# The convolution's second transform on four quarters of TensorE, with K's exchanged rows copied inside SBUF

## The chip, the cores and the metric

The kernel runs on one core of one Trainium2 chip. The metric is the time of one execution on the device in microseconds (us); lower is better. A core has a matrix engine (TensorE, PE in the profile, with its weight loads listed apart as PEld), a vector engine (VectorE, DVE), a scalar engine (ScalarE, ACT), a GpSimd engine (POOL) and a sync engine (SyncE, SP) that here only issues transfers. They share an on-chip memory of 128 partitions (SBUF). TensorE writes into a second, small memory of eight banks (PSUM), from which VectorE and ScalarE read. Transfers run on 16 DMA engines; SP, ACT and POOL each have a queue to issue them from.

## The reference, cut to what matters

Two mixers see the same `x` (2048 x 448) and are blended by a gate. One is a long convolution with a kernel K built from a state-space model; the other is attention within four segments of 512 rows, with a memory carried between segments.

```python
P = jnp.exp((A * dt[:, None])[:, :, None] * pos[None, None, :])
K = 2.0 * jnp.einsum("dn,dnl->dl", C, P).real          # 448 x 2048
Kf = jnp.fft.rfft(K, L2); Uf = jnp.fft.rfft(u_t, L2)   # L2 = 4096
y = jnp.fft.irfft(Uf * Kf[None, :, :], L2)[:, :, :L]
a = y + u * D_skip
...                                                     # b: attention, 16 heads of 28, 4 segments
return g * a + (1 - g) * b
```

All arithmetic is float32.

## The kernel before, in words

The first half (to about 445 us) builds K, projects q, k and v, and takes the first of two transform stages for u. The second half (`second_half`, L1206) runs the attention and, stirred into it, the rest of the convolution.

The 4096-point transform is split into two factors. The first factor leaves, in DRAM, two arrays `GU` and `GK` of 64 blocks; a block has 64 rows (real and imaginary part of 32 points) of 448 channels. `convolve` (L569) takes them through the second factor, multiplies the spectra and goes back through the inner factor of the inverse. It works in 32 chunks of two blocks, 128 rows, and has three kinds of step:

- **T**, `transform(c)`: K's chunk. Two products, one for each block, each with a 64 x 128 matrix out of `cf` and 64 x 448 data, into one PSUM buffer of two banks. ScalarE copies all 128 x 896 to `ks`. The 128 columns hold each output row twice, the second time with real and imaginary part exchanged (for K: imaginary, real, and so on), since a complex product needs both.
- **P**, `product(c)`: the same with u's chunk (real, imaginary, real, imaginary), and VectorE multiplies the PSUM buffer by `ks` into `pr` (128 x 896).
- **B**, `back(c)`: for two chunks, four products with 128 x 64 matrices out of `cb`; ScalarE copies the result to `bs`, and ACT's queue writes it to `BB` in DRAM, from where `finish` takes it at the end.

A float32 product appears in the trace as two matmul instructions. A matmul on fewer than 128 rows or columns uses a part of the array, its `tile_position`; T and P use two halves of 64 rows, B two halves of 64 columns.

The order on TensorE is written out: `mm` (L1378) keeps program order. `second_half` walks over 16 groups `i` (four segments times four groups of heads), each in six rounds `r` (L1261 to L1316). A round issues a few dummy matmuls in rounds 3, 4 and 5 (`WARM`: 1, 3, 3 of them, output `ps_pv<-wz`), one step of the next group's score maxima (`maxima`, L974; called M below), one step of this group's scores and exponentials (`weigh`, L1008; W), in round 1 the product with the values (`ps_pv<-PT,V`) and a transposition, after each segment steps of `seg_end` (L1147), which ends with 128 x 448 products by `wo`, and last some steps of `convolve`: for i from 1 to 12 an account grows by `RATIO` = 1.15 a round, and each whole unit is one step (T, P or B). What is left after i = 12 runs at once. M, W, T, P and B all draw their PSUM buffer from one ring of three (`ps("a")`, two banks each): a new one waits until the buffer three before it has been read. VectorE reads M's and P's, ScalarE W's, T's and B's. The scores come in three shapes: rounds 0 and 1 have 512 columns, 2 and 3 have 384 + 128, 4 and 5 have 256.

The order on the other engines and queues is chosen by a planner that simulates the program; only some SP transfers are tied behind others: the loads of `skip` (`xt`) behind the latest load of `gu` (`late`, `ldma`, L1408 to L1416). Loads of `gk` and `gu` come from SP through a ring of four buffers each; `cf` and `cb` are loaded once for four chunks, two buffers each.

Of the kernel before, what the change touches and what calls it, by code (L numbers as in the profile page):

```python
# [12 lines left out]
F32 = mybir.dt.float32  # L13
# [3 lines left out]
AF = mybir.ActivationFunctionType  # L17
ALU = mybir.AluOpType
# [5 lines left out]
D = 448  # L24
# [15 lines left out]
def host_consts():  # L40
# [3 lines left out]
    e = np.zeros((2, 64, 3, 512), np.float32)  # L44
    w = np.zeros((16, 3, 16, 64), np.float32)
# [3 lines left out]
    w = np.zeros((16, 3, 16, 32), np.float32)  # L49
# [4 lines left out]
    w = np.zeros((8, 2, 3, 2, 8, 32), np.float32)  # L54
# [20 lines left out]


    lane = np.arange(32)
    fw = np.zeros((64, 2, 32, 6, 32))
    bk = np.zeros((64, 4, 32, 2, 32))
    for k1 in range(64):  # L80
        k = k1 + 128 * lane
# [20 lines left out]
        f[:, :, 2:] = f[:, :, [0, 1, 1, 0]]  # L102
    fw = fw.reshape(32, 128, 192).transpose(1, 0, 2)
    bk = bk.reshape(64, 128, 64).transpose(1, 0, 2)


    f = np.stack([2 * np.cos(ang.T), -2 * np.sin(ang.T)], 1) / 4096
# [460 lines left out]

def convolve(nc, k, fp):  # L569

    NC = 32
    KB = 4
    cf, cb, gk, gu, ks, pr = {}, {}, {}, {}, {}, {}
    rows = lambda t, c: t[2 * c : 2 * c + 2].rearrange("s r n d -> (s r n) d")

    def load(c):
        if c >= NC:
            return
        if c % KB == 0:
            cf[c // KB] = fp.tile([128, KB, 192], F32, tag="cf", name="cf", bufs=2)  # L580
            k.dma(cf[c // KB], k.c_fw[:, c : c + KB])
            cb[c // KB] = fp.tile([128, 2 * KB, 64], F32, tag="cb", name="cb", bufs=2)
            k.dma(cb[c // KB], k.c_bk[:, 2 * c : 2 * c + 2 * KB])
# [5 lines left out]
    def second(c, x, o):  # L589

        pt = k.ps("a")
        w = cf[c // KB]
# [5 lines left out]
    def transform(c):  # L598
        pt = second(c, gk.pop(c), 64)
        ks[c] = fp.tile([128, 2, D], F32, tag="ks", name="ks", bufs=3)  # L600
        nc.scalar.activation(ks[c], pt, AF.Copy)

    def product(c):
        pt = second(c, gu.pop(c), 0)
        pr[c] = fp.tile([128, 2, D], F32, tag="pr", name="pr", bufs=3)
        nc.vector.tensor_tensor(pr[c], pt, ks.pop(c), ALU.mult)  # L606

    def back(c):

        pt = k.ps("a")  # L610
        for i in range(2):
            for s in range(2):
                k.mm(
                    pt[64 * s : 64 * s + 64, i, :D], cb[c // KB][:, 2 * ((c + i) % KB) + s], pr[c + i][:, s],
                    start=True, stop=True, tile_position=(0, 64 * s),
                )
            pr.pop(c + i)
        bs = fp.tile([128, 2, D], F32, tag="bs", name="bs", bufs=2)
        nc.scalar.activation(bs, pt[:, :, :D], AF.Copy)
        k.adma(k.BB[2 * c : 2 * c + 4].rearrange("(i s) r n d -> (s r n) i d", i=2), bs)  # L620

    for c in range(3):
        load(c)
    yield
    for c in range(NC + 2):
        load(c + 3)
        if c < NC:
            transform(c)
        yield
        if 1 <= c <= NC:  # L630
            product(c - 1)
            yield
        if c >= 2 and c % 2 == 1:
            back(c - 3)
            yield


# [983 lines left out]
```

## Time and profile before

| What | Value |
|---|---|
| time, median of 3 runs | 852.42 us (850.0 to 855.2) |
| span of the profiled execution, first to last instruction | 850.4 us |
| PE busy in the span | 750.1 us, 88% |
| DVE, ACT, POOL busy | 582.0, 538.6, 171.8 us |
| instructions | 19021 |
| first step T to last step B of the convolution | about 491 to 750 us |

The profiled execution's own time, apart from its span, is not listed; its span lies within the range of the times. "Busy" is the union of an engine's instructions. Matmuls overlap in the pipeline, so the distance between the starts of two blocks, not the length of one record, is what a block costs. In rows of the timeline the first number is the start in us, the second the length; a bracket gives the idle time of that engine before it and what ended it. In groups, `x` is the count, after the bar stand the busy time (us), the mean of one (ns), and the idle time before.

### The profile page before, as it was taken

The page shows a single profiled execution, that of the slowest core. Times are in us where ns is not written, and L with a number is a line of the kernel's source. Part 1 is how long each engine was busy: PE and PEld are TensorE (multiplying, and loading weights), DVE is VectorE, ACT ScalarE, POOL GpSimd, SP SyncE. Part 2 cuts the span into 40 slices and gives each one's busy share as a digit, 9 for nine tenths or more (in the row PEclk, how much of TensorE's full clock was granted, in tenths as well). Part 3 has the DMA queues.
Part 4 walks back from the last instruction along what each step waited for, and adds up shares of the span by engine and source line. Part 5 has one row for each costly group of instructions (what it writes and reads, how often), then busy time and mean ns, then how long its engine had stood idle before and what let it go on. Part 6 is the DMA issues. An engine that isn't in the chain of part 4 may idle for free.

```text
span 850.4 us, 19021 instructions
## 1 busy us (share of the span) xinstructions
PE 750.1 (88%) x7608; PEld 405.1 (48%) x7608; DVE 582.0 (68%) x1143; ACT 538.6 (63%) x638; POOL 171.8 (20%) x217
## 2 busy tenths in 40 slices
PE   1686987998879989899988999989997998988997
PEld 1363655764546655566643444434443444343443
DVE  8878678767788676876687765656565757563474
ACT  4867889799998989898863255554453444521320
POOL 5314111011110111001110121341115113331110
PEclk9589999999999989799999899999999999979899
DMA  9347853325642346314558967667466645654872
GB/s 248 91 108 237 247 186 112 99 91 172 197 143 85 104 153 200 132 46 149 178 202 349 349 221 235 204 220 233 118 219 220 194 152 182 210 205 152 223 231 97
DMA packets 88290, 152.98 MB, mean 180 GB/s; under 512 B 20626, under 2 KB 57162, under 8 KB 88154
## 3 DMA queue, kind: packets, MB, share of 16 engines
q1 hardware_dynamic: 79130, 140.83, 51.7%
q10 hardware_dynamic: 7424, 9.18, 3.1%
q0 software_dynamic: 1648, 1.76, 0.8%
q8 instruction: 60, 0.98, 0.5%
q14 instruction: 28, 0.23, 0.1%
HBM read 90.87 MB, written 60.63 MB: 178 GB/s over the span
## 4 chain that ended last, share of the span: by engine, by line
PE 54%; ACT 16%; DVE 15%; DMA 7%; issue 6%; POOL 1%; SPq 1%; ACTq 0%; DVEq 0%; POOLq 0%
PE ps_a L1379 19%; PE ps_m L1379 17%; PE ps_pv L1379 8%; ACT cs L1344 7%; PE ps_arg L1379 5%; PE ps_k L1379 3%; DVE jk L994 3%; DVE Y L397 2%; ACT L1344 2%; PE ps_m L1382 2%; DVE Y L398 1%; DVE X L393 1%; DMA xt<-in_A_u 1%; ACT EX L1344 1%; DMA ident<-in_c_id 1%
## 5 line engine op out<-in xcount | busy, mean ns | idle before, releaser
L994 DVE CUSTOM_DVE_ANT_0 jk<-ps_a,mk 128x512 f32<-128x512 f32 (+3 forms) x256 | 124.9, 488 | 71.0 <-PE ps_a L1379 63.7
L1024 ACT ACTIVATE PT<-ps_a 128x1024 f32<-128x1024 f32 (+1 forms) x96 | 84.5, 881 | 118.6 <-PE ps_a L1379 112.0
L359 POOL TENSOR_TENSOR EX<-EX,cab 128x1024 f32<-128x1024 f32 x28 | 53.5, 1913 | 309.1 <-ACT EX L1344 244.8
L1344 ACT ACTIVATE cs<-ps_arg 128x1024 f32<-128x1024 f32 x111 | 107.3, 1021 | 0.6 <-DVE Y L398 0.3
L1379 PE MATMUL ps_m<-xh,w 112*128 112x512 f32 x256 | 92.9, 412 | 0.4 <-DVE lo L765 0.4
L1379 PE MATMUL ps_a<-qu,ku 32*128 32x512 f32 (+3 forms) x768 | 89.3, 353 | 1.7 <-DVE mx L994 1.4
L1035 POOL TENSOR_SCALAR_AFFINE_SELECT PT<-PT 128x256 f32<-128x256 f32 (+1 forms) x96 | 46.5, 485 | 206.5 <-ACT PT L1024 206.4
L393 DVE TENSOR_TENSOR X<-EX,cs 128x1024 f32<-128x1024 f32 x56 | 68.3, 1220 | 25.4 <-ACT cs L1344 25.4
L1379 PE MATMUL ps_k<-Y,X 128*32 128x64 f32 x3584 | 64.1, 226 | 9.0 <-DVE Y L398 8.8
L1379 PEld LDWEIGHTS ps_k<-Y,X 128*32 128x32 f32 x3584 | 54.9, 113 | 35.2 <-DVE Y L398 16.1
L397 DVE TENSOR_TENSOR Y<-EY,cs 128x1024 f32<-128x1024 f32 x56 | 70.0, 1250 | 0.0
L1379 PEld LDWEIGHTS ps_a<-qu,ku 32*128 32x128 f32 x768 | 62.4, 194 | 12.4 <-DVE mx L994 4.7
L1344 ACT ACTIVATE cs<-cs,bhp 128x1024 f32<-128x1024 f32 x56 | 64.5, 1151 | 1.8
L399 DVE SCALAR_TENSOR_TENSOR Y<-EY,cs 128x512 f32<-128x512 f32 x56 | 41.0, 732 | 31.2 <-ACT cs L1344 29.1
L1344 ACT ACTIVATE EY<-ps_arg 128x1024 f32<-128x1024 f32 x52 | 53.1, 1031 | 11.1 <-PE ps_arg L1379 10.1
L1379 PEld LDWEIGHTS ps_m<-xh,w 112*128 112x128 f32 x256 | 48.0, 188 | 19.7 <-issue 7.6
L1379 PE MATMUL ps_a<-ku,qu 32*128 32x512 f32 (+3 forms) x256 | 46.0, 394 | 12.3 <-DVE mx L994 9.9
L1379 PE MATMUL ps_arg<-ct,lh 64*128 64x512 bf16 x224 | 43.6, 387 | 9.0 <-ACT cs L1344 5.7
L1379 PE MATMUL ps_m<-xl,w 112*128 112x512 f32 x128 | 50.3, 393 | 0.0
L1379 PEld LDWEIGHTS ps_a<-ku,qu 32*128 32x128 f32 x256 | 22.2, 189 | 58.7 <-DVE mx L994 27.0
L1379 PEld LDWEIGHTS <-lh 64*128 64x128 bf16 x392 | 22.2, 95 | 53.4 <-issue 39.8
L606 DVE TENSOR_TENSOR pr<-ps_a,ks 128x896 f32<-128x896 f32 x32 | 34.8, 1087 | 17.7 <-PE ps_a L1379 17.0
(212 smaller groups left out, 1395.3 us busy)
## 6 DMA issues: line engine op xcount, KB each, us to landing
w<-WD SPq DMA_DIRECT2D x32, 448.0 KB, 4.7
qu<-QD SPq DMA_DIRECT2D x16, 512.0 KB
ku<-KD SPq DMA_DIRECT2D x16, 512.0 KB
GU<-gs SPq DMA_DIRECT2D x32, 224.0 KB, 2.5
GK<-gs SPq DMA_DIRECT2D x8, 896.0 KB, 5.1
gk<-GK SPq DMA_DIRECT2D x32, 224.0 KB, 4.7
gu<-GU SPq DMA_DIRECT2D x32, 224.0 KB, 3.7
BB<-bs ACTq DMA_DIRECT2D x16, 448.0 KB, 2.6
```

The source lines that it names most:

```text
L359: nc.gpsimd.tensor_tensor(o, o, cab, ALU.mult)
L393: v.tensor_tensor(X, ex, t[:, :, 0], ALU.mult)
L397: v.tensor_tensor(Y[:, :, :, :32], lo, y[:, :, :, ::-1], ALU.mult)
L398: v.tensor_tensor(Y[:, 0, :, 32:], ey[:, :, 32:], y[:, 0], ALU.mult)
L399: v.scalar_tensor_tensor(Y[:, 1, :, 32:], ey[:, :, 32:], -1.0, y[:, 1], ALU.mult, ALU.mult)
L606: nc.vector.tensor_tensor(pr[c], pt, ks.pop(c), ALU.mult)
L994: v.tensor_tensor_reduce(junk[:, :n], pt[:, x, o : o + n], k.mk[:, SEG - n :], 1.0, -3e38, ALU.add, ALU.max, mx[:, 3 - t, h : h + 1],)
L1024: nc.scalar.activation(PT[:, 2 * hp : 2 * hp + 2, 512 * b : 512 * b + n], pt[:, :, :n], AF.Exp, scale=SCALE)
L1035: nc.gpsimd.affine_select(sl, sl, pat, ALU.is_ge, 0.0, base=0, channel_multiplier=-1)
L1344: x = op(*args, **kw)
L1379: tc.keep_in_program_order(nc.tensor.matmul(*args, **kw))
L1382: tc.keep_in_program_order(nc.tensor.transpose(*args))
```

## The change

T and P take two chunks at a time (`m` of 16 instead of `c` of 32) and make each output row once. The matrix is now 64 x 64, and the four products (two row halves `s`, two chunks `i`) each sit on one quarter of the array, at (64 s, 64 i). The result, for two chunks, fills one PSUM buffer as one chunk's did.

Since the exchanged rows of K are no longer made by TensorE, T copies the PSUM buffer into half 0 of `ks`, and two transfers from ACT's queue move it inside SBUF into half 1 with neighbouring partitions exchanged (even rows to odd ones, odd to even). P reads its PSUM buffer twice: two multiplications on VectorE, by half 0 and half 1. B takes `pr` in those halves: eight products of 64 x 64 on four quarters, two accumulated into each output, where there were four of 128 x 64.

`gk` and `gu` come as 16 loads of twice the size each, through rings of two; they are issued after P instead of at the start of a turn. `cf` has a third of the bytes. `ks` and `pr` have rings of two double-size buffers. The steps are 49 instead of 83, and `RATIO` is 0.68 instead of 1.15, so that they spread over the same rounds. The rest of the program, the dummies included, is untouched.

```diff
-    fw = np.zeros((64, 2, 32, 6, 32))
+    fw = np.zeros((64, 2, 32, 2, 32))
...
-    rows = lambda t, c: t[2 * c : 2 * c + 2].rearrange("s r n d -> (s r n) d")
+    rows = lambda t, m: t[4 * m : 4 * m + 4].rearrange("(i s) r n d -> (s r n) i d", i=2)
+    halves = [slice(0, 64), slice(64, 128)]
...
-        gk[c] = fp.tile([128, D], F32, tag="gk", name="gk", bufs=4)
-        k.dma(gk[c], rows(k.GK, c))
-        gu[c] = fp.tile([128, D], F32, tag="gu", name="gu", bufs=4)
-        k.late(k.dma(gu[c], rows(k.GU, c)))
+        gk[m] = fp.tile([128, 2, D], F32, tag="gk", name="gk", bufs=2)
+        k.dma(gk[m], rows(k.GK, m))
+        gu[m] = fp.tile([128, 2, D], F32, tag="gu", name="gu", bufs=2)
+        k.late(k.dma(gu[m], rows(k.GU, m)))
...
-        for s in range(2):
-            r = slice(64 * s, 64 * s + 64)
-            k.mm(pt[:, s, :D], w[r, c % KB, o : o + 128], x[r], start=True, stop=True)
+        for s, r in enumerate(halves):
+            for i, o in enumerate(halves):
+                k.mm(
+                    pt[o, s, :D], w[r, 2 * (m % 2) + i], x[r, i],
+                    start=True, stop=True, tile_position=(64 * s, 64 * i),
+                )
...
-        nc.scalar.activation(ks[c], pt, AF.Copy)
+        nc.scalar.activation(ks[m][:, 0], pt, AF.Copy)
+        x = ks[m].rearrange("(e a) b s d -> a e b s d", a=2)
+        for a in range(2):
+            k.adma(x[a, :, 1], x[1 - a, :, 0])
...
-        nc.vector.tensor_tensor(pr[c], pt, ks.pop(c), ALU.mult)
+        x = ks.pop(m)
+        for b in range(2):
+            nc.vector.tensor_tensor(pr[m][:, b], pt, x[:, b], ALU.mult)
...
-        for i in range(2):
-            for s in range(2):
-                k.mm(
-                    pt[64 * s : 64 * s + 64, i, :D], cb[c // KB][:, 2 * ((c + i) % KB) + s], pr[c + i][:, s],
-                    start=True, stop=True, tile_position=(0, 64 * s),
-                )
+        for b in range(2):
+            for i, r in enumerate(halves):
+                for s, o in enumerate(halves):
+                    k.mm(
+                        pt[o, i, :D], w[r, b, s], x[r, b, s],
+                        start=(b == 0), stop=(b == 1), tile_position=(64 * i, 64 * s),
+                    )
...
+    for m in range(NM + 2):
+        if m < NM:
+            transform(m)
             yield
+        if 1 <= m <= NM:
+            product(m - 1)
+            load(m + 1)
+            yield
+        if m >= 2:
+            back(m - 2)
             yield
...
-RATIO = 1.15
+RATIO = 0.68
```

More of the change, by code (lines that the diff above doesn't have):

```diff
@@ new lines, in transform, with product @@
+    def transform(m):
+        pt = second(m, gk.pop(m))
+        ks[m] = fp.tile([128, 2, 2, D], F32, tag="ks", name="ks", bufs=2)
+        nc.scalar.activation(ks[m][:, 0], pt, AF.Copy)
+        x = ks[m].rearrange("(e a) b s d -> a e b s d", a=2)
+        for a in range(2):
+            k.adma(x[a, :, 1], x[1 - a, :, 0])
+    def product(m):
+        pt = second(m, gu.pop(m))
+        pr[m] = fp.tile([128, 2, 2, D], F32, tag="pr", name="pr", bufs=2)
+        x = ks.pop(m)
+        for b in range(2):
+            nc.vector.tensor_tensor(pr[m][:, b], pt, x[:, b], ALU.mult)
@@ L622, in convolve @@
-    for c in range(3):
-        load(c)
+        k.adma(k.BB[4 * m : 4 * m + 4].rearrange("(i s) r n d -> (s r n) i d", i=2), bs)
+    load(0)
+    load(1)
     yield
[L625 to L631, printed above, removed]
-            yield
-        if c >= 2 and c % 2 == 1:
-            back(c - 3)
+    for m in range(NM + 2):
+        if m < NM:
+            transform(m)
+            yield
+        if 1 <= m <= NM:
[4 more added lines that the diff above has]
+            back(m - 2)
```

37 lines of the change are left out of this document (14 added, 23 removed).

## The prediction

> **What bounds the kernel now.** I read the page first: the span, the engines, and TensorE's granted clock in 40 slices of 21.3 us.
>
> ```profile
> span 850.4 us, 19021 instructions
> ...
> PE 750.1 (88%) x7608; PEld 405.1 (48%) x7608; DVE 582.0 (68%) x1143; ACT 538.6 (63%) x638; POOL 171.8 (20%) x217
> ...
> PEclk9589999999999989799999899999999999979899
> ```
>
> TensorE (PE) is the busiest, and from slice 24 on, where the convolution's steps lie (490 to 750 us), its clock is nearly always full. So the second view is that stretch alone: busy time by engine (PE, PEld, DVE, ACT, POOL in this order), then the chain that ended last, then PE's own waits.
>
> ```profile
> 490.00:750.00 260.00, 244.28 (x1746) 109.58 (x1744) 156.18 (x469) 124.00 (x151) 71.95 (x123) 0.97 0.61 197
> ...
> by line: PE ps_a L1379 42.2%; PE ps_pv L1379 16.0%; PE ps_m L1379 11.1%; DVE jk L994 4.1%; issue 4.0%; DMA xt<-in_A_u 3.7%; DMA r<-RD 2.2%; DMA dn<-pvs 2.0%; PE ps_m L1382 1.8%; DMA RD<-rs 1.6%; DMA qu<-mn 1.6%; POOL xt L1122 1.5%; DVE xt L
> ...
> PE ps_a L1379 <- DVE mx L994: 10.1, 10, 3.5
> PE ps_a L1379 <- DVE pr L606: 2.9, 6, 1.3
> ```
>
> PE is busy for 244.3 of 260 us, VectorE (DVE) for 156.2, ScalarE (ACT) for 124.0. The chain runs over PE for 42.2 + 16.0 + 11.1 + 1.8 = 71% of the stretch. What PE lost to VectorE is 10.1 + 2.9 = 13.0 us. TensorE is the limit here, and time taken from it should come back unless something else is late next. The groups by shape tell what the convolution costs, in order of cost: score maxima (`jk`), the multiplication (L606), the matmuls of T (`gk`) and B (`pr`; P's are as many as T's), and ScalarE's copy (L601).
>
> ```profile
> L994 DVE CUSTOM_DVE_ANT_0 jk<-ps_a,mk 128x512 f32<-128x512 f32 x64 | 44.0, 687 | 14.6 <-PE ps_a L1379 13.2
> ...
> L994 DVE CUSTOM_DVE_ANT_0 jk<-ps_a,mk 128x384 f32<-128x384 f32 x64 | 35.5, 554 | 30.1 <-PE ps_a L1379 28.4
> ...
> L606 DVE TENSOR_TENSOR pr<-ps_a,ks 128x896 f32<-128x896 f32 x32 | 34.8, 1087 | 17.7 <-PE ps_a L1379 17.0 <-ACT PT L1024 0.7
> ...
> L1379 PE MATMUL ps_a<-gk,cf 64*128 64x448 f32 x128 | 34.2, 612 | 2.0 <-DVE pr L606 1.3 <-DVE mx L994 0.2
> ...
> L1379 PE MATMUL ps_a<-pr,cb 128*64 128x448 f32 x128 | 30.0, 593 | 1.7 <-DVE pr L606 1.5
> L601 ACT ACTIVATE ks<-ps_a 128x896 f32<-128x896 f32 x32 | 29.3, 917 | 13.6 <-PE ps_a L1379 13.1 <-PE ps_pv L1379 0.5
> ...
> L994 DVE CUSTOM_DVE_ANT_0 jk<-ps_a,mk 128x256 f32<-128x256 f32 x64 | 27.0, 422 | 24.3 <-PE ps_a L1379 22.1 <-DVE mx L994 0.5
> ...
> L994 DVE CUSTOM_DVE_ANT_0 jk<-ps_a,mk 128x128 f32<-128x128 f32 x64 | 18.4, 288 | 2.0
> ```
>
> And the timeline gives the distance from one block to the next on PE:
>
> ```profile
> 596.73 0.18 PEld L1379 LDWEIGHTS ps_a<-ku,qu 32*128 32x128 f32 x2 [0.65 <-issue]
> ...
> 597.75 3.27 PE L1379 MATMUL ps_m<-wo,pvs 128*128 128x448 f32 x8
> ...
> 612.83 0.33 PEld L1379 LDWEIGHTS <-wz 128*128 128x128 bf16 x3 [0.65 <-issue]
> ...
> 613.58 0.18 PEld L1379 LDWEIGHTS ps_a<-ku,qu 32*128 32x128 f32 x2 [0.42 <-issue]
> ...
> 614.13 0.30 PEld L1379 LDWEIGHTS ps_a<-gk,cf 64*128 64x128 f32 x4
> ...
> 615.09 0.18 PEld L1379 LDWEIGHTS ps_a<-ku,qu 32*128 32x128 f32 x2 [0.65 <-DVE mx L994]
> ...
> 617.16 0.50 PE L1379 MATMUL ps_a<-ku,qu 32*128 32x512 f32 x2
> ...
> 618.13 2.36 PE L1379 MATMUL ps_pv<-PT,V 128*32 128x512 f32 x32
> ...
> 620.95 1.72 PE L1379 MATMUL ps_a<-pr,cb 128*64 128x448 f32 x8
> ...
> 622.61 0.18 PEld L1379 LDWEIGHTS ps_a<-ku,qu 32*128 32x128 f32 x2 [0.70 <-issue]
> ...
> 623.67 0.37 ACTq L620 DMA_DIRECT2D BB<-bs  x1
> ...
> 624.08 1.02 ACT L1024 ACTIVATE PT<-ps_a 128x1024 f32<-128x1024 f32 x1 [0.44 <-PE ps_a L1379]
> ```
>
> A T runs from 614.13 to the next block's weight load at 615.09: 0.96 us. Its record, four matmul instructions, shows that both 64-row halves run together: four of mean 612 ns fit into that distance. B takes 620.95 to 622.61, 1.66 us. A round's M and W take 617.16 to 618.13 = 0.97 us with 512 columns, 596.73 to 597.75 = 1.02 us with 384 + 128, and 613.58 to 614.13 = 0.55 us with 256; three dummies take 612.83 to 613.58 = 0.75 us.
>
> **The change, part by part.**
>
> *T and P on quarters.* 128 instructions of `gk`, four to a block, are 32 T's, and the 32 multiplications are 32 P's: 64 blocks. 32 remain, of eight instructions each. If four quarters run abreast as two halves do, a block keeps its 0.953 us (0.96 here, 0.95 for a P), and 32 x 0.953 = 30.5 us go. The trace has halves abreast by rows (T) and by columns (B), and no block with both; the bounds of the gain are 30.5 us, and for two abreast 64 x 0.953 - 32 x 1.70 = 6.6 us (a block of 2 x 0.75 us of streaming, 0.75 being the 0.95 less 0.2 of lead-in, and that 0.2). I take 30.5, since the halves in both directions show no loss.
>
> *B on quarters.* Sixteen instructions instead of eight, four abreast instead of two: the same 1.66 us, nothing changed; two abreast, they would stream 2.9 us instead of 1.46, 16 x 1.46 = 23 us more.
>
> *ScalarE.* 16 copies of 917 ns go (-14.7 us) and 32 transfers to issue come. The one that it issues now, `BB<-bs`, takes 0.37 us at 623.67, and the next instruction starts 0.41 us after it: 32 x 0.41 = 13.1 us. The sum is nothing, and ScalarE's idle 136 us cover it. Behind the two issues waits the next exponential, 0.82 us instead of the 0.92 of a copy that is gone. If the second transfer had to wait for the first to land, ScalarE would stand 2.6 us (landing of `BB<-bs`, an estimate for the exchange) 16 times; its idle time is 8.5 us to each of the 16 turns, so that too would be hidden mostly. Taken at nothing, between -1.6 us (the difference of the two sums) and +42 (16 x 2.6).
>
> *Transfers.* The exchange moves 16 x 448 KB inside SBUF. P needs it four steps after T, at 0.68 a round 5.9 rounds; 72 rounds in 260 us are 3.6 us each, so 21 us. The transfers of now, with KB each and us to landing:
>
> ```profile
> gk<-GK SPq DMA_DIRECT2D x32, 224.0 KB, 4.7
> gu<-GU SPq DMA_DIRECT2D x32, 224.0 KB, 3.7
> BB<-bs ACTq DMA_DIRECT2D x16, 448.0 KB, 2.6
> ```
>
> A load of `gk` can go once the T two turns back has read its buffer, a load of `gu` once its P has, with three steps (16 us) to spare; SP has 32 fewer issues, and queued behind them are the loads of `qu` and `ku` for later groups. At nothing: the cover is 16 us or more, against landings of 2.6 to 4.7. Were it gone, each turn would wait such a landing, 16 x 2.6 = 42 us and more.
>
> *VectorE, and the ring of three buffers.* VectorE's work is unchanged, 32 multiplications of 1087 ns, but they now come in pairs on one PSUM buffer. What that hold does is seen here:
>
> ```profile
> 542.42 1.09 DVE L606 TENSOR_TENSOR pr<-ps_a,ks 128x896 f32<-128x896 f32 x1 [0.38 <-PE ps_a L1379]
> ...
> 543.57 0.65 PE L1379 MATMUL ps_a<-gk,cf 64*128 64x448 f32 x2 [0.36 <-DVE pr L606]
> ```
>
> The multiplication ends at 543.51 and the T that wanted its buffer starts at 543.57. A multiplication starts some 0.25 us after PE has left P, so a P's buffer is free about 1.4 us after it now, and 0.25 + 2 x 1.12 = 2.5 us after it in the change (1.12 with the distance to the next). PE in the meantime does one M and W (0.55 to 1.02 us) and any dummies, and the third buffer drawn is P's. Then the next W wants the buffer of an M whose maxima VectorE could only start after the pair (1.44 us for 512 columns, 1.77 for 384 + 128, 0.93 for 256, from the groups with 0.05 us between). With RATIO 0.68 the n-th step falls in round n / 0.68, rounded up, and P of turn k is step 3k + 2 (the first is 3), which places all 16. Seven lie in quiet groups i, where no other work lies between: after P0 and P3 (round 4, a step follows) 0.75 + 0.55 us of PE work stand against 2.5, loss 1.2 each; P1 (round 1) 1.5; P8 (round 2) 1.2; P2 (round 5, no step in the next round) 1.5 for the buffer and 1.2 for the maxima behind it, 2.7; P14 (round 4, none next) 1.2 + 0.7 = 1.9; P13 (round 0) none, the values' product and the transposition, 618.13 to 620.95 = 2.8 us, cover it. Sum 9.7 us. The other nine lie in groups with segment ends, where blocks of `wo` (3.27 us at 597.75) or the waits of the next part cover them: nothing. Bounds: nothing, and 16 x 2.7 = 43 us.
>
> In sentences apart: the Trainium skill, TensorEngine Tiling (Array Packing), section Performance Considerations, says that tiling speeds up TensorE and not the reading of PSUM, which may become the bottleneck after it. By that rule the upper bound is the nearer one, and the rival "hold" below results; the groups above (VectorE idle for 104 of 260 us) bear it out in part only.
>
> *Stretches that PE doesn't set.* In four places the chain leaves PE for transfers of a segment's end (`xt`, `dn`, then `RD` and `r`). One piece of the first, then PE's work on `cf` in each of the four (four instructions to a block):
>
> ```profile
> 550.06 5.47 DMA xt<-in_A_u
> ...
> 549.70:565.30 15.60, 4.93 (x16) 1.41 (x16) 0.89 0.75 257
> 639.10:650.60 11.50, 3.07 (x12) 0.90 (x12) 1.00 0.78 270
> 711.30:720.80 9.50, 2.05 (x8) 0.60 (x8) 0.93 0.39 122
> 738.40:752.20 13.80, 1.53 (x4) 0.30 (x4) 0.88 0.39 128
> ```
>
> 16 + 12 + 8 + 4 instructions are 10 of the 64 blocks; their share, 10 / 64 x 30.5 = 4.8 us, is not gained. 0 to 10 us (10 if shorter rounds uncover as much again). In the first, `xt` is held behind a `gu` load that comes earlier now; up to 2 us less, not counted.
>
> *The clock.* PE is granted half speed in stretches of 3.41 us after a stretch in which it did little:
>
> ```profile
> 644.37:647.78 3.41, 1.98 (x13) 0.64 (x11) 1.64 (x8) 1.02 (x1) 1.65 (x2) 1.00 1.05 385
> 647.78:651.19 3.41, 1.24 (x12) 0.76 (x14) 3.38 (x8) 0.60 (x1) 3.41 (x4) 1.00 0.37 137
> 651.19:654.60 3.41, 3.41 (x10) 0.75 (x6) 0.14 (x2) 0.92 (x1) 1.66 (x4) 0.51 0.24 41
> ```
>
> 1.98 us of work in the first stretch left the clock at 1.00 in the second, the 1.24 us of the second let it fall to 0.51 in the third. Half speed for 3.41 us costs up to 1.7 us. The stalls of 2.7 and 1.9 us above leave 0.7 and 1.5 us of work, below or at that edge, those of 1.2 don't: 2 x 1.7 = 3.4 us. Bounds: 0, and 16 x 1.7 = 27 us. By the Trainium skill (TensorE: Matmul & The Clock Gate, Part 1) it takes an idle window of about 3.4 us to halve the clock, and this term would be nothing, the sum 837; the trace disagrees, with half speed after a stretch with 1.24 us of work.
>
> *Sum.* 850.4 - 30.5 + 9.7 + 4.8 + 3.4 = 837.8 us of span. The median of the runs is 2.0 us above the profiled span (852.4 against 850.4), so I predict 840 us, 1.5% less.
>
> **The rivals.**
>
> *All of the saving arrives.* VectorE is idle 40% of the stretch, and PE's waits for single products were 2.9 us; if the planner lets other maxima go between the pair, terms of 9.7 and 3.4 vanish: 850.4 - 30.5 + 4.8 + 2 = 827 us. Against it: 542.42 shows a step that waits for one product already.
>
> *The hold eats it (slower).* If each P costs PE on average more than (30.5 - 4.8) / 16 = 1.6 us, nothing is gained. At the 2.7 us of a P without a step behind it, half of them with a half-speed stretch, it is 852.4 - 30.5 + 4.8 + 43 + 14 = 884 us at the far end; at 2.2 us and five such stretches, 852.4 - 25.7 + 35 + 8.5 = 870. I put this case at 855 to 872. For it: without the 30.5 us VectorE's 156 us stand against 230 instead of 260, 68%, and its work comes in lumps.
>
> *The quarters don't run four abreast.* T and P give only 6.6 us, and B costs 23 more: 852.4 - 6.6 + 23 = 869 us, the stalls being covered by the longer blocks.
>
> *The exchange blocks ScalarE or comes late.* At the 2.6 us of a landing in each turn, 852.4 - 25.7 + 42 = 869 us. Against it: 16 us or more of cover.
>
> **How the numbers follow.** Forecast (832 to 848): 0.35. All of it arrives (823 to 832): 0.21. The hold eats it: 0.24, of which 0.08 near 852. Not four abreast: 0.07. Exchange: 0.06. The rest, 0.07, is small losses around no change. About 0.5% (4.3 us) is what a measurement of this kernel can tell from no change: faster 0.55, same 0.14, slower 0.31. The range 824 to 869 leaves out 1 in 10 at each end; the likeliest case's own is 832 to 848.
>
> **What would show it.** T, P and B of about 0.95, 0.95 and 1.66 us with 8, 8 and 16 matmul records each; the exchange landed before P; PE waiting for `pr` some 1.2 us after a P and for `mx` once behind it; half speed in quiet groups only behind stalls of 1.9 us and more. It is wrong if a T takes 1.7 us, if PE's waits on `pr` and `mx` come to more than 30 us between 490 and the last B, or if ScalarE's exponentials wait for a transfer.

## The result, and the profile after

The changed kernel takes 862.4 us (median of 4 runs, 859.58 to 864.83) where the kernel before, run beside it, takes 851.62: a ratio of 1.0124 (95% interval 1.0082 to 1.0167), 1.2% slower, about 10.6 us. I had predicted 840 us, 1.5% faster.

First the page of the changed kernel: span, engines, and TensorE's granted clock in 40 slices.

```profile
span 857.9 us, 19214 instructions
...
PE 736.7 (86%) x7736; PEld 400.1 (47%) x7736; DVE 581.9 (68%) x1143; ACT 524.4 (61%) x622; POOL 171.2 (20%) x217
...
PEclk9998999999999989899999989989996997878799
```

TensorE is busy for 13.4 us less (750.1 before) and the span is 7.5 us longer. Next the convolution's stretch, 475 to 775 us, in one row each: busy time of PE, PEld, DVE, ACT and POOL, then the mean granted clock. First the kernel before:

```profile
475.00:775.00 300.00, 279.20 (x1942) 127.29 (x1942) 179.80 (x547) 137.15 (x167) 78.90 (x136) 0.94 0.64 210
```

and the kernel after:

```profile
475.00:775.00 300.00, 257.57 (x2049) 117.64 (x2049) 175.88 (x545) 120.22 (x148) 77.19 (x133) 0.90 0.68 227
```

PE is busy for 21.6 us less, and all of that is idle time now: 42.4 us instead of 20.8. The clock fell from 0.94 to 0.90, so by estimate some 12 us more of the 300 were lost to half speed (300 x 0.04); what PE still does takes longer for it. VectorE and ScalarE have no more to do than before.

The steps themselves came out as the prediction had them. Groups by shape, kernel after:

```profile
L613 DVE TENSOR_TENSOR pr<-ps_a,ks 128x896 f32<-128x896 f32 x32 | 33.3, 1082 | 13.9 <-PE ps_a L1387 9.5 <-ACT mn L1012 3.3 <-ACT PT L1032 1.0
...
L1387 PE MATMUL ps_a<-gk,cf 64*64 64x448 f32 x128 | 16.5, 587 | 1.0 <-PE ps_a L1387 1.0
```

T's matmuls fell from 34.2 us to 16.5 with the same count of instructions: the four quarters run abreast. Now the timeline of a T and a P in a quiet group, kernel after (start, length, engine; the bracket is the idle time before and what ended it):

```profile
524.10 0.98 PE L1387 MATMUL ps_a<-gk,cf 64*64 64x448 f32 x8
...
525.01 0.33 PEld L1387 LDWEIGHTS <-wz 128*128 128x128 bf16 x3 [0.70 <-issue]
...
525.14 0.92 ACT L603 ACTIVATE ks<-ps_a 128x896 f32<-128x896 f32 x1 [0.34 <-PE ps_a L1387]
...
526.09 1.13 ACTq L606 DMA_DIRECT2D ks<-ks  x2
...
526.33 0.98 PE L1387 MATMUL ps_a<-gu,cf 64*64 64x448 f32 x8
...
527.27 0.60 ACT L1032 ACTIVATE PT<-ps_a 128x512 f32<-128x512 f32 x1 [1.21 <-PE ps_a L1387]
...
527.45 2.09 DVE L613 TENSOR_TENSOR pr<-ps_a,ks 128x896 f32<-128x896 f32 x2 [0.36 <-PE ps_a L1387]
527.92 0.53 PEld L1387 LDWEIGHTS ps_a<-qu,ku 32*128 32x128 f32 x6 [0.50 <-ACT PT L1032]
...
529.68 0.49 PE L1387 MATMUL ps_a<-ku,qu 32*128 32x512 f32 x2 [0.79 <-DVE pr L613]
...
530.93 0.96 PE L1387 MATMUL ps_a<-qu,ku 32*128 32x512 f32 x6 [0.76 <-DVE mx L1002]
```

A T costs PE 0.91 us (524.10 to 525.01) and does two chunks. But ScalarE, which ends the copy at 526.06, issues two transfers until 527.22 and only then turns to the exponential of a block that lay ready: PE's next W waits for that buffer (0.50). Then the pair of multiplications, 527.45 to 529.54, makes PE wait 0.79 us for `pr` and 0.76 for `mx`. PE's waits from 490 to 755 us, in all, how often, longest:

```profile
PE ps_a L1387 <- DVE mx L1002: 20.9, 14, 5.0
...
PE ps_a L1387 <- DVE pr L613: 4.3, 5, 1.1
PE ps_a L1387 <- ACT PT L1032: 4.2, 6, 1.7
```

Before, those for `mx` and `pr` were 10.1 and 2.9, and exponentials (`PT`) were not among what PE's matmuls waited for; its weight loads waited 1.4 us for them, and 7.6 now. The longest wait, 5.0 us, lies at a segment's end, here in the kernel after:

```profile
641.32 0.54 POOL L1107 DMA_DIRECT2D dn<-pvs  x1 [1.70 <-ACT pvs L1063]
...
642.90 0.29 DVE L1002 CUSTOM_DVE_ANT_0 jk<-ps_a,mk 128x128 f32<-128x128 f32 x1
...
648.74 0.55 DVE L1072 RECIPROCAL rc<-dn 128x64 f32<-128x64 f32 x1 [5.54 <-DMA dn<-pvs]
...
649.70 0.55 DVE L1002 CUSTOM_DVE_ANT_0 jk<-ps_a,mk 128x384 f32<-128x384 f32 x1
...
651.58 0.58 PE L1387 MATMUL ps_a<-ku,qu 32*128 32x256 f32 x2 [5.00 <-DVE mx L1002]
```

VectorE stands 5.54 us at the reciprocal `rc`, until its denominators `dn` have landed. The maxima that come behind it in VectorE's order, whose scores PE has long written, start only then (649.70), PE fills the ring of three buffers and stands too.

### The profile page after: what moved, and what is told of

Its sections match the earlier page's. It is cut to its first block, busy times and chain, and to the rows that moved or that the text cites. A ratio compares the mean times of both kernels' runs of the same rounds, so it can differ in the third digit from the quotient of the medians.

```text
span 857.9 us, 19214 instructions
## 1 busy us (share of the span) xinstructions
PE 736.7 (86%) x7736; PEld 400.1 (47%) x7736; DVE 581.9 (68%) x1143; ACT 524.4 (61%) x622; POOL 171.2 (20%) x217
## 4 chain that ended last, share of the span: by engine, by line
PE 51%; ACT 17%; DVE 14%; DMA 7%; issue 7%; POOL 1%; ACTq 1%; SPq 0%; DVEq 0%; POOLq 0%
PE ps_a L1387 17%; PE ps_m L1387 16%; PE ps_pv L1387 8%; ACT cs L1352 7%; PE ps_arg L1387 5%; DVE jk L1002 4%; PE ps_k L1387 3%; PE ps_m L1390 2%; ACT L1352 2%; DMA dn<-pvs 2%; DVE Y L396 2%; DMA w<-WD 1%; DMA WD<-wsp 1%; ACT EX L1352 1%; DMA ident<-in_c_id 1%
## 5 line engine op out<-in xcount | busy, mean ns | idle before, releaser
L1387 PE MATMUL ps_a<-qu,ku 32*128 32x512 f32 (+3 forms) x768 | 91.1, 359 | 14.3 <-DVE mx L1002 10.4
L398 DVE SCALAR_TENSOR_TENSOR Y<-EY,cs 128x512 f32<-128x512 f32 x56 | 38.9, 695 | 31.4 <-ACT cs L1352 30.1
L1387 PEld LDWEIGHTS ps_m<-xh,w 112*128 112x128 f32 x256 | 48.0, 188 | 20.8 <-issue 7.6
L1387 PE MATMUL ps_pv<-PT,V 128*32 128x128 f32 (+3 forms) x512 | 46.2, 510 | 0.0
```

The costliest lines, as they stand in the source:

```text
L398: v.scalar_tensor_tensor(Y[:, 1, :, 32:], ey[:, :, 32:], -1.0, y[:, 1], ALU.mult, ALU.mult)
L1387: tc.keep_in_program_order(nc.tensor.matmul(*args, **kw))
```

## The experiments

Ratios are to the kernel before on the same chip, with 95% intervals; a difference between two kernels of different rows is worked out from their ratios. The theory after this reading was that PE was never the sole limit: its chain and the loop over VectorE's maxima are about equally long. The rivals were single costs of the change: the exchange's issue on ScalarE, the hold of P's buffer, the clock, the segment ends. The first group asks what PE's time is worth, the second takes the change's parts one by one, the third mends the segment ends in both kernels, the fourth asks what is left.

| Kernel | Ratio | Interval |
|---|---|---|
| after | 1.0124 | 1.0082 to 1.0167 |
| b1, before, T and P over half the columns | 0.9982 | 0.9937 to 1.0028 |
| c2, before, half the maxima | 0.9936 | 0.9901 to 0.9971 |
| c1, both of these | 0.9831 | 0.9775 to 0.9888 |
| a1, after, exchange issued by SP | 0.995 | 0.9922 to 0.9977 |
| a2, after, one multiplication | 0.9883 | 0.9833 to 0.9932 |
| a4, after, dummies behind P | 1.0015 | 0.9981 to 1.0048 |
| v1, a1 and a4 | 0.9996 | 0.9956 to 1.0036 |
| v3, a1, multiplications split with GpSimd | 1.0108 | 1.0032 to 1.0183 |
| d0, before, late divide | 0.9888 | 0.9836 to 0.994 |
| d1, a1, late divide | 0.9858 | 0.9794 to 0.9923 |
| e2, d0 with b1's half columns | 0.9885 | 0.9821 to 0.995 |
| e1, d1, one multiplication | 0.9633 | 0.9568 to 0.9699 |
| f2, d1, second multiplication from SBUF | 0.9876 | 0.9825 to 0.9926 |
| f3, d1, with a copy by ScalarE | 0.9943 | 0.9905 to 0.9981 |
| f4, f3, second multiplication on GpSimd | 0.9887 | 0.9816 to 0.9958 |
| f5, d1, second multiplication without the hold | 0.9851 | 0.9799 to 0.9903 |
| f6, d1, hold without the second multiplication | 0.9679 | 0.9604 to 0.9754 |

**What PE's time is worth.** b1 is the kernel before with less streaming in T and P:

```diff
-            k.mm(pt[:, s, :D], w[r, c % KB, o : o + 128], x[r], start=True, stop=True)
+            k.mm(pt[:, s, :224], w[r, c % KB, o : o + 128], x[r, :224], start=True, stop=True)
```

> The kernel before, with T's and P's matmuls over 224 of the 448 columns (the other half of the spectra is left out, the copies and multiplications read the half twice and keep their length). It takes away PE time alone, 64 blocks x 0.37 us = 24 us, with single products, no exchange and the old RATIO. Theory 'PE was the bound': 850 - 24 + 4 (stretches that PE doesn't set) and a few us of half clock, 830 to 838 us. Rival 'PE was not the bound, or the clock falls with any time taken from it': 845 to 853 us.

Some 24 us of PE's work went, and the time stayed: 0.9982. The stretch from the first T to the last B, columns as above, first before and then b1:

```profile
490.92:748.36 257.44, 241.91 (x1733) 108.86 (x1733) 154.84 (x463) 123.25 (x150) 70.20 (x119) 0.97 0.61 198
492.30:751.15 258.85, 229.42 (x1732) 112.39 (x1733) 155.50 (x464) 122.42 (x150) 70.57 (x119) 0.92 0.61 198
```

PE is busy for 12.5 us less, not 24, since the clock is 0.92 instead of 0.97, and it is idle for 13.9 us more. So the saving went in about equal parts to waiting and to a lower clock. c2 takes VectorE's maxima over the last half of the columns instead, where there are more than 128; c1 does both.

```diff
-                        junk[:, :n], pt[:, x, o : o + n], k.mk[:, SEG - n :], 1.0, -3e38,
+                        junk[:, :h], pt[:, x, o + n - h : o + n], k.mk[:, SEG - h :], 1.0, -3e38,   # h = max(n // 2, 128)
```

> The kernel before with half the columns of the score maxima left out (29 us of VectorE between 490 and 750 us), PE's work untouched. Theory 'two chains of the same length': at most the 13 us that PE waits for VectorE, 0.985 to 0.995 of the kernel before. Theory 'VectorE alone sets the pace': 0.965 to 0.98. Theory 'PE alone': 0.995 to 1.00.

> The kernel before with two things left out: half the columns of T's and P's matmuls (24 us of PE, as in the run with half columns, which was worth nothing) and half the columns of the score maxima on VectorE where there are more than 128 (0.27, 0.20 and 0.13 us of 0.69, 0.55 and 0.42, some 29 us of VectorE between 490 and 750 us; the mask is raised by a constant so that the exponentials stay finite). Theory 'two chains of the same length' (PE's order, and the loop from a matmul of the maxima over VectorE back to the buffer ring): with both shortened the time falls by 20 us or more, to 0.965 to 0.98 of the kernel before. Theory 'clock' (any time taken from PE comes back as half speed and waits for transfers): 0.985 to 1.00.

c2 gains 0.6%, but in its profile hardly here: its first T and its last B,

```profile
485.69 1.02 PE L1380 MATMUL ps_a<-gk,cf 64*128 64x448 f32 x4 [0.45 <-DMA gk<-GK]
...
741.70 3.26 PE L1380 MATMUL ps_a<-pr,cb 128*64 128x448 f32 x8
```

lie 256.0 us apart, those of the kernel before

```profile
490.92 1.02 PE L1379 MATMUL ps_a<-gk,cf 64*128 64x448 f32 x4 [0.20 <-DVE mx L994]
...
748.36 1.72 PE L1379 MATMUL ps_a<-pr,cb 128*64 128x448 f32 x8
```

257.4. Those of c1, both edits,

```profile
488.57 0.65 PE L1381 MATMUL ps_a<-gk,cf 64*128 64x224 f32 x4 [0.44 <-DMA gk<-GK]
...
736.01 3.10 PE L1381 MATMUL ps_a<-pr,cb 128*64 128x448 f32 x8
```

are 247.4 apart, and b1's 258.9. Neither PE's time alone nor VectorE's alone is worth more than 1.4 us in this stretch; taken away together they are worth 10 (one profile each, c1's of a run 4.8 us under its median). In the ratios it shows less clearly: b1 and c2 multiplied give 0.9918, c1 has 0.9831, 0.9% less, where the three intervals together leave 0.8% open. c1 also missed both ranges that I had set (0.965 to 0.98, and 0.985 to 1.00 for the clock). What these runs say is that PE's chain and the round trip of a score block (PE writes it, VectorE takes its maxima, the buffer returns to PE through a ring of three) are about equally long. How much of the loss is the waiting itself and how much the lower clock that comes with it, no run separates.

**The change's parts.** a1 issues the exchange from SP: `k.adma(x[a, :, 1], ...)` becomes `k.dma(x[a, :, 1], ...)`.

> The changed kernel with one edit: the two exchange transfers of each turn are issued from SP's queue instead of ACT's. Theory 'issue': ScalarE stands 1.2 us between the end of the copy to ks and the next exponential (1.2 to 2.2 us in the trace, 20 us in all), PE's waits on ACT PT rose from 1.4 to 11.8 us because of it, and they go: about 852 us, 8 to 12 below the changed kernel. Theory 'hold' (VectorE's pair of multiplications keeps the PSUM buffer) and theory 'clock': no change, 860 to 864 us.

From 1.0124 to 0.995, some 14.8 us (0.0174 x 852). ScalarE in a1, at the same T:

```profile
524.50 0.92 ACT L603 ACTIVATE ks<-ps_a 128x896 f32<-128x896 f32 x1 [0.34 <-PE ps_a L1387]
525.78 0.60 ACT L1032 ACTIVATE PT<-ps_a 128x512 f32<-128x512 f32 x1 [0.36 <-PE ps_a L1387]
```

The exponential starts 0.36 us after the copy, where it was 1.21 in the kernel after. PE's matmuls no longer wait for exponentials (4.2 us in the kernel after), and its weight loads 1.7 us instead of 7.6. So the two issues of each turn cost the change more than its whole loss of 10.6 us. a2 leaves P's second multiplication out (B takes half 0 twice):

```diff
-        for b in range(2):
-            nc.vector.tensor_tensor(pr[m][:, b], pt, x[:, b], ALU.mult)
+        nc.vector.tensor_tensor(pr[m][:, 0], pt, x[:, 0], ALU.mult)
```

> The changed kernel without P's second multiplication: B reads the first product in place of the second, so half of the complex product is left out; everything else, the exchange included, stays. A P then holds its PSUM buffer for 1.1 us instead of 2.2, and VectorE has 17 us less to do. Theory 'hold': the 9.7 us of stalls and the half-speed stretches behind them go, 845 to 851 us. Theory 'issue': nothing but VectorE's slack changes, 858 to 863 us.

It gives 2.4% against the kernel after. a4 puts three dummy matmuls behind each P (`turn_over(3)` after its step), so that PE has work while the pair holds the ring; v1 is a1 and a4 together.

> The changed kernel with three dummy matmuls (0.64 us of streaming) issued behind each P in groups 1 to 12, where PE stalls for the P's buffer anyway: 16 x 0.64 = 10 us of PE time. Theory 'clock': the half-speed time after 440 us falls from 78 us towards the 47 of the kernel before, and the time falls by 5 to 12 us, to 850 to 857. Rival (the half speed is a by-product and sits where PE waits anyway): 862 to 870 us.

> The changed kernel with both edits that helped alone: exchange issued from SP's queue, and three dummies behind each P. If they act on different things (ScalarE's wait, and the clock), their gains of 1.7 and 1.1% add: 0.98 to 0.988 of the kernel before. If both only shift the same waits: 0.992 to 1.00.

With the exchange on ACT the dummies gain 1.1%; with it on SP they lose 0.5%, the intervals just overlapping. So the gains of a1 and a4 (1.7 and 1.1%) do not add; which wait covers which was not traced. a2's does: it is 2.4% here, and 2.3% with the exchange on SP and the segment ends mended (e1 below). v3 is a1 with ScalarE copying P's buffer to SBUF (`us`), VectorE multiplying half 0 from there and GpSimd half 1.

> The changed kernel with the exchange issued from SP and P split over three engines: ScalarE copies P's PSUM buffer to SBUF (0.92 us, then the buffer is free), VectorE multiplies by half 0 and GpSimd by half 1, both from SBUF. The buffer is held 1.2 us instead of 2.5 and VectorE has 17 us less to do; ScalarE has 15 us more. Theory 'hold': as the run without the second product, and SP's gain on top, 0.975 to 0.985 of the kernel before. If ScalarE's order is what PE waits for: 0.995 or more.

It lost 1.6% against a1, and its groups say why:

```profile
L615 POOL TENSOR_TENSOR pr<-us,ks 128x896 f32<-128x896 f32 x16 | 39.7, 2484 | 17.4 <-ACT us L612 13.5 <-issue 1.5 <-DMA ks<-ks 1.4
...
L614 DVE TENSOR_TENSOR pr<-us,ks 128x896 f32<-128x896 f32 x16 | 32.9, 2054 | 12.2 <-ACT us L612 12.0
```

VectorE needs 2054 ns on average for a multiplication that takes 1082 from PSUM, so one costs nearly as much as two did.

**The segment ends.** d0 is the kernel before with two instructions of VectorE moved: the reciprocal comes two steps after its transfers are issued and behind the newest maxima, and the last segment's multiplication of `xt` comes three rounds after its loads, also behind the newest maxima. d1 is a1 with the same edit.

```diff
-        inverse(dn[:, :f], 0, h0, h1, r8[s], queue)
+        for _ in range(2):
+            yield
+        inverse(dn[:, :f], 0, h0, h1, r8[s], queue)
...
-        v.reciprocal(rc[:, :f], x)
+        with k.issue_after(k.last_max.ins):
+            v.reciprocal(rc[:, :f], x)
```

> The kernel before, with VectorE's instructions that wait for a transfer at a segment's end (the reciprocal `rc` of the denominators, and the last segment's multiplication of `xt`) put two rounds later and behind the newest maxima, so that no maxima are queued behind such a wait. Theory (TensorE and the loop of maxima over the three PSUM buffers are about equally long, and the ends of segments add stalls in which VectorE stands at a transfer): TensorE's four gaps there, 9.3 us in the profile of the kernel before, go, with up to 8 us of half speed behind them, and nothing takes their place; 4 to 10 us less, ratio 0.988 to 0.995. Rival (those gaps are slack that comes back as waits for maxima in the following rounds, as the 24 us of the half-column kernel did): 0.998 to 1.002.

> The changed kernel with the exchange issued by SP, and with the same two instructions of VectorE put later. With TensorE needing less for T and P, VectorE meets these waits earlier and TensorE stands longer there: 17 us of gaps in the four places with the exchange on SP. Theory (segment ends are where a good part of the change's saving is lost): the gain over the same kernel without the edit (0.995 of the kernel before) is larger than the edit's gain in the kernel before: 8 to 15 us less, ratio 0.977 to 0.986. Rival (the saving is lost in every group to the ring of three buffers and the clock, segment ends only being where it shows): the gain is no larger than in the kernel before, ratio 0.988 to 0.996.

d0 gains 1.1%, d1 0.9% against a1. d1's 0.9858 lies at the edge of what the theory had for it, but the gain is no larger than in the kernel before, as its rival had it. Each gain is uncertain by 0.5 to 0.7%; within that, what the segment ends cost was there before the change, and the change made it little worse. PE's waits in d0 (from 490 to 755 us):

```profile
PE ps_a L1386 <- DVE pr L606: 6.0, 10, 1.7
PE ps_a L1386 <- DVE mx L994: 5.2, 13, 0.8
```

The wait for `mx` is half of the 10.1 us of the kernel before, its longest 0.8 instead of 3.5; that for `pr` rose from 2.9 to 6.0, so a part of the saving comes back there. In d1 the reciprocal at the segment end shown above waits 1.31 us instead of 5.54:

```profile
641.66 0.55 DVE L1073 RECIPROCAL rc<-dn 128x64 f32<-128x64 f32 x1 [1.31 <-DMA dn<-pvs]
```

d1, 839.7 us, is the fastest whole kernel of this study, d0 at 841.94 next to it; their ratios overlap, so with both repairs the change itself is worth 0.3%, which can't be told from nothing. e2 asks whether PE's time is worth something now: d0 with b1's half columns.

> The kernel before with VectorE's two instructions at segment ends put later (0.9888 alone), and with the matmuls of T and P over 224 of 448 columns, which takes about 24 us of TensorE's work away and nothing of any other engine's. Theory one (TensorE's time was worth nothing in the half-column kernel since VectorE's waits at segment ends took it): now it is gained, 10 to 20 us more, ratio 0.965 to 0.977. Theory two (TensorE and the loop of maxima over three buffers are about equally long in every group, wherever VectorE waits): as without the half columns, 0.984 to 0.993.

0.9885 against 0.9888: nothing still. So it was not the segment ends that ate b1's 24 us. Its waits:

```profile
PE ps_a L1387 <- DVE mx L995: 11.4, 27, 1.5
PE ps_a L1387 <- DVE pr L607: 6.0, 10, 1.8
```

27 waits for maxima instead of 13, all short. The stretch from the first T to the last B, d0 and then e2:

```profile
488.51:735.97 247.46, 231.40 (x1719) 106.04 (x1733) 152.63 (x460) 123.28 (x150) 69.75 (x119) 1.00 0.63 207
486.65:744.25 257.60, 231.03 (x1718) 114.59 (x1732) 151.94 (x460) 122.47 (x150) 70.07 (x119) 0.91 0.61 198
```

PE is busy as long as in d0 though some 24 us of its work are gone, since its clock is 0.91 instead of 1.00, and it is idle for 10.5 us more. The two profiles lie apart by more than the kernels do (they are of runs of 839.6 and 848.4 us, the medians 841.94 and 846.45), but the mean granted clock of all runs fell too, from 0.964 to 0.949, by estimate some 13 us of 850. So the saving is given back all along, in many short waits and in a clock that fell with them.

**What is left.** e1 is d1 without P's second multiplication.

> The changed kernel with the exchange on SP, VectorE's two instructions at segment ends put later, and P's second multiplication left out (B reads half 0 twice), so that VectorE has 16 multiplications of 128x896 less and holds P's buffer once. Against the kernel with the first two edits (0.9858 of the kernel before). Theory (with the exchange and the segment ends out of the way, the pair of multiplications and VectorE's load are what is left between the change and its saving): another 2 to 3%, ratio 0.957 to 0.970. Rival (the rest is TensorE's order itself, the clock's half-speed stretches and the rounds of maxima without a convolution step, which the pair doesn't set): 0.974 to 0.986.

It gains 2.3% more, 19 us, so the pair stands between the change and its saving. It costs in two ways: it holds P's buffer twice as long (the term of my prediction), and it takes 16 x 1.09 = 17.4 us of VectorE's time. f2 to f6 separate the two. f2 and f5 keep the load without the hold: the second multiplication reads SBUF alone. In f2 it is half 0 of `ks` by half 1, in f5 half 0 by itself, put behind the first.

> The changed kernel with the exchange on SP and VectorE's two instructions at segment ends put later (0.9858 of the kernel before), and P's second multiplication fed from SBUF: it multiplies half 0 of `ks` by half 1 in place of the PSUM buffer by half 1, so the result is another, VectorE has as many instructions of the same shape, and the buffer is free after the first. Leaving the second one out gave 0.9633. Theory one (what is left of the loss is the hold: the buffer kept by two multiplications): 0.958 to 0.972. Theory two (it is VectorE's load: the time of a multiplication on an engine that is itself about as long as TensorE): 0.978 to 0.992.

f2 gives 0.9876, no gain, but it is not clean: its second multiplication comes late in VectorE's order and VectorE stands before it for 19.3 us in all.

> The changed kernel with the exchange on SP and VectorE's two instructions at segment ends put later; P's second multiplication is half 0 of `ks` by itself, so the result is another, it reads SBUF alone, waits for no exchange, and comes behind the first in VectorE's order. VectorE's load as with the pair, P's buffer held by one multiplication. With the pair 0.9858, without the second multiplication 0.9633. If the load decides: 0.977 to 0.990. If the hold decides: 0.958 to 0.971. If both together are needed for the loss: near the second of these; if either is enough: near the first.

f5 gives 0.9851, the same as the pair (0.9858); its load is 3 us above the pair's (16 x 0.2, by the mean below), too little for the 2.2%. Its group, the one multiplication that makes the 3 us (the other fifteen took 1.08 us), and PE's waits:

```profile
L614 DVE TENSOR_TENSOR pr<-ks 128x896 f32<-128x896 f32 x16 | 20.6, 1286 | 0.0
...
555.38 4.36 DVE L614 TENSOR_TENSOR pr<-ks 128x896 f32<-128x896 f32 x1
```

```profile
PE ps_a L1395 <- DVE mx L1003: 21.1, 26, 4.9
...
PE ps_a L1395 <- DVE pr L612: 1.2, 4, 0.4
```

In d1 they were

```profile
PE ps_a L1394 <- DVE mx L1002: 11.9, 22, 2.0
PE ps_a L1394 <- DVE pr L613: 7.5, 7, 1.5
```

Without the hold the waits for `pr` are gone, from 7.5 us to 1.2, and those for `mx` have nearly doubled: PE waits for VectorE all the same, only at another buffer. (The longest, 4.9 us, stands behind the multiplication of 4.36 us; without it the waits for `mx` are still 16.2 us.) f6 is the opposite: one multiplication, put behind a copy of the buffer by ScalarE, so that it is held as long as by the pair.

```diff
+        us = fp.tile([128, 2, D], F32, tag="us", name="us", bufs=1)
+        nc.scalar.activation(us, pt, AF.Copy)
+        nc.vector.tensor_tensor(pr[m][:, 0], pt, x[:, 0], ALU.mult)
```

> The same two edits, P's second multiplication left out (B reads half 0 twice), and in its place a copy of the buffer by ScalarE (0.92 us) that the one multiplication is put behind, as the trace of the kernels with such a copy shows; nothing reads the copy. The buffer is held as long as by the pair, about 2.4 us, and VectorE has 16 multiplications less; ScalarE has 15 us more. If the load decides: 0.958 to 0.971. If the hold decides, or either is enough: 0.977 to 0.990.

0.9679, close to e1's 0.9633, the intervals overlapping. Its waits:

```profile
PE ps_a L1395 <- DVE mx L1003: 9.6, 19, 1.9
PE ps_a L1395 <- DVE pr L614: 8.1, 9, 1.3
```

The waits for `pr` are as in d1 (8.1), and most of the time is gained. So VectorE's load is enough for the loss; whether the hold, or ScalarE's copies, cost something beside it (0.5% by the two ratios, from nothing to over 1% by their intervals) f6 leaves open. f3 and f4 tried to use this with the whole computation: ScalarE's copy, VectorE's first multiplication from PSUM, the second from the copy, on VectorE in f3 and on GpSimd in f4.

> The same two edits, and P's buffer also copied to SBUF by ScalarE (`us`, 16 copies of about 0.92 us); VectorE's first multiplication reads PSUM, the second the copy. The whole computation. The buffer is held by one multiplication and a copy beside it. Theory one (the hold): 0.962 to 0.978. Theory two (VectorE's load): 0.982 to 0.998, since nothing is taken from it and ScalarE gets 15 us more.

> As the kernel with ScalarE's copy, and the second multiplication, which reads the copy, on GpSimd (2.48 us each in the earlier run that used it). The whole computation. The load and the hold are both gone from VectorE. If its first multiplication, which reads PSUM and SBUF, keeps its 1.09 us: 0.962 to 0.976. If it takes the 2.05 us that VectorE's multiplication took when both its operands lay in SBUF and GpSimd worked beside it: 0.985 to 1.0.

f3 takes nothing from VectorE, its second multiplication even takes 1538 ns on average, and it gains nothing (0.9943, a loss against d1). f4 takes the load away and still gives 0.9887. Its multiplications:

```profile
L615 POOL TENSOR_TENSOR pr<-us,ks 128x896 f32<-128x896 f32 x16 | 33.5, 2095 | 7.9 <-ACT us L613 6.5 <-DMA ks<-ks 1.4
...
L614 DVE TENSOR_TENSOR pr<-ps_a,ks 128x896 f32<-128x896 f32 x16 | 17.4, 1090 | 9.8 <-ACT us L613 9.7
```

VectorE's kept its 1090 ns, so by the condition that I had set it should have gained. It also waited for ScalarE's copy before it started (9.7 us), which I had not foreseen, but f6 does that too. What differs between f4 and f6 is GpSimd's 33.5 us and B's need of their result; which of these costs the 2% was not tried. PE's waits for `mx` and `pr` are nearly the same (11.2 and 8.4 us against 9.6 and 8.1), those for the exponentials that GpSimd masks are 3.2 us instead of 0.6. So taking the load from VectorE did not pay here when GpSimd took it over, and why is open.

## Why the prediction went wrong

**The step that failed** is the sentence "TensorE is the limit here, and time taken from it should come back unless something else is late next". The term of 30.5 us was right as work: T, P and B came out at 0.91, 0.92 and 1.66 us from weight load to weight load, with 8, 8 and 16 matmul records. But b1 and e2 show that 24 us of PE's time, taken without any other edit, bring nothing. A busy share of 94% and 71% of the chain made PE look like the only limit; the loop over VectorE was about as long. Where PE is shortened, it waits, and its clock falls: in b1 13.9 us more idle, and 12.5 us less busy instead of 24. It was partly in the views: VectorE idle 40% of the stretch was taken for slack, though what it waited for was PE and what PE waited for next would be its maxima. I had the rival ("VectorE's 156 us stand against 230 instead of 260, 68%, and its work comes in lumps") at 0.24. The time fell into its range, 855 to 872 us, in part by luck: its price was the held buffer, and what the runs show is VectorE's time and ScalarE's issues.

**ScalarE, "taken at nothing".** It measured 14.8 us (a1), the largest single cost after the pair's. The length was of the right size (1.16 us for two issues, where I had 0.82); the cover was wrong. I hid the issues in ScalarE's idle 136 us, but they stand between a copy and an exponential whose PSUM buffer PE needs in the same round. My bounds, -1.6 to +42, held it. None of the exponentials waited for a transfer, as the prediction asked for; they waited for the issuing of one.

**The hold, 9.7 us.** The place was right (PE waits 0.79 for `pr` and 0.76 for `mx` behind the P at 526.33, where I had 1.2 in all), but the cause was in the main not the buffer. The pair costs 19 us (e1). f5, with the load and without the hold, has this cost, and f6, with the hold and without the load, has little of it (0.5%, uncertain by 1%), so it is VectorE's time: "VectorE's work is unchanged" was true and beside the point, since it counts in full once PE is no longer ahead. In a sentence apart: by the Trainium skill, TensorEngine Tiling (Array Packing), section Performance Considerations, tiling speeds up TensorE and not the emptying of PSUM, which may become the bottleneck; e1 against d1, 2.3%, bears that out here, with VectorE's time and not the buffer as what binds.

**Segment ends, 4.8 us.** The mechanism, stretches that PE doesn't set, was right; PE's longest wait there went from 3.5 us to 5.0. Mending them is worth 0.9 to 1.1% in either kernel (d0, d1), so it is in the main a cost of both and not of the change.

**The clock, 3.4 us.** About 12 us by the two rows of 475 to 775. Two stretches of the kernel after:

```profile
529.12:532.53 3.41, 2.10 (x16) 0.98 (x20) 3.12 (x9) 1.49 (x2) 0.41 (x1) 1.00 0.93 332
532.53:535.94 3.41, 3.41 (x31) 1.30 (x23) 0.00 (x0) 0.69 (x2) 0.41 (x1) 0.51 0.42 161
```

2.10 us of work in the first let the clock fall to 0.51 in the one after it, where 1.98 us in the prediction's row had left it at 1.00. So PE's busy time in one stretch does not decide it alone, and the edge by which I sorted the stalls is not one; what decides stays open. In steps of 3.41 us, 18 stretches between 475 and 775 us ran at half speed and 10 before the change: eight more, at up to 1.7 us each, where I had counted two. The Trainium skill, TensorE: Matmul & The Clock Gate, Part 1, halves the clock after an idle window of about 3.4 us; this trace shows it after a window that was more than half busy.

**Transfers at nothing** was right: no multiplication waited for the exchange, though one of its transfers takes 4.5 us to land.

```profile
ks<-ks ACTq DMA_DIRECT2D x32, 224.0 KB, 4.5
```

The range held the time, by its upper end; the signs I had named for being wrong (waits on `pr` and `mx` over 30 us, a T of 1.7) would not have told: 20.9 + 4.3 = 25.2 us. Last, the sum itself was at fault: I added terms, and v1 shows that waits in such a loop need not add.

## To carry to other kernels

Before crediting time taken from the busiest engine, halve that engine's work in a throwaway kernel: if the time stays, as in b1, something else is as long, here the loop through VectorE, and c1 gained only by shortening both. A transfer's issue on a computing engine costs whatever waits behind it in that engine's order, not the engine's idle share (14.8 us here, with 136 us idle). Put an instruction that waits for a transfer behind the work that is ready: here this gained about 1% in either kernel by moving two instructions.

## What the runs showed of the hardware that I had not expected

A multiplication of 128 x 896 on VectorE took 1082 to 1091 ns on average with one operand in PSUM, beside GpSimd's 2095 ns multiplication too (f4). With both operands in SBUF it took the same 1.08 us in fifteen of f5's sixteen cases; the mean of 1286 comes from the one of 4.36 us, which began while GpSimd multiplied `xt`. In v3, whose mean is 2054, the engine that began later took longer:

```profile
643.01 2.11 POOL L615 TENSOR_TENSOR pr<-us,ks 128x896 f32<-128x896 f32 x1 [0.63 <-ACT us L612]
643.03 3.03 DVE L614 TENSOR_TENSOR pr<-us,ks 128x896 f32<-128x896 f32 x1 [1.25 <-ACT us L612]
```

At 520.49, where VectorE began first, it took 1.09 us and GpSimd 2.99. The Trainium skill, SBUF — State Buffer, section SBUF: two separate sides, says that a VectorE instruction with two SBUF inputs and a GpSimd instruction that reads SBUF take a shared pair of ports in turn; the figures of f4, f5 and v3 agree with it.

Two readers of one PSUM buffer on different engines ran one after the other in f3, f4 and f6: VectorE's multiplication was released by the end of ScalarE's copy (`<-ACT us`, 9.7 us of waiting in f4). Whether the chip or the program's own ordering asks for that, no run here tells.
